# One-token attention with a 32768-long cache beside a SwiGLU FFN: own space for the projection weights, a broadcast q, earlier weight loads, and most of the output projection moved ahead

## The chip, the cores and the metric

The kernel runs on one core of one Trainium2 chip. The metric is the device time of one execution in microseconds (us), as a median over several executions. The profile is one execution, taken by the hardware profiler; its span is 1 to 2 us shorter than the timed figure. Engines in the profile: PE is TensorE (PEld its weight loads), DVE is VectorE, ACT is ScalarE, POOL is GpSimd, SP is SyncE, which here issues all transfers ("SPq" is its queue).

## The reference

One token, 32 heads with a K and a V cache of 32768 x 128 each in bf16, and a small FFN on the same normalised input:

```python
xn = _layernorm(x)                                   # x: [1, 1, 640]
q = (xn @ wq)                                        # wq: [640, 4096], 32 heads of 128
scores = einsum("bhqd,bhkd->bhqk", q, k) * 128**-0.5  # k, v: [1, 32, 32768, 128]
p = softmax(scores); o = einsum("bhqk,bhkd->bhqd", p, v)
att = o.reshape(1, 1, 4096) @ wo                     # wo: [4096, 640]
ffn = (silu(xn @ w_gate) * (xn @ w_up)) @ w_down     # 640 -> 1728 -> 640
out = x + att + ffn
```

K and V are 537 MB together, the weights 17 MB: 554 MB have to be read once.

## The kernel before

A head's K and V lie with 256 positions on each of 128 partitions. K comes in four chunks of 2 MB a head, into a ring of `KR = 6` slots; V in eight of 1 MB, into a ring of `VR = 8`. VectorE does q.k: a multiply with q broadcast over partitions, a tree of four folding additions in place, and a reduce. POOL reduces the maximum and the sum over partitions (a "partition all-reduce" each) and scales the maximum between the two, ScalarE takes exp, TensorE multiplies V (as weights) by p ("PV"). When a head's PV and its 1/sum are there, ScalarE copies the result out of PSUM, scaled by 1/sum (the "eviction").

```python
for i in range(NKC):                                  # VectorE; NKC = 128 chunks
    ...
    v.wait_ge(kdma[slot].sem, 16 * (i // KR + 1))
    dve_t.inc(v.tensor_tensor(out=kr, in0=kr, in1=qbh[...].to_broadcast(...), op=ALU.mult))
    for w in TREE:                                    # 64, 32, 16, 8
        ...
        dve_t.inc(v.tensor_tensor(out=kr[:, :, 0:w], in0=kr[:, :, 0:w], in1=kr[:, :, w:2 * w], op=ALU.add))
    v3 = dve_t.inc(v.tensor_reduce(out=scs[...], in_=kr[:, :, 0:TREE[-1]], axis=AX.X, op=ALU.add))
    if c == NCK - 1:
        head_ops(h)                                   # maximum of the head
        if h >= 1: rz_op(h - 1)                       # 1 / sum of the head before
        ...
```

wq and wo have no space of their own: wq lies in the first K slots at the start, wo in the same slots at the end. The in-order transfer queue shows what that means:

```python
wq_v = kflat[:, 0:NC_D * HQ * DH]...;  wo_v = kflat[:, 0:H * D]...     # kflat is the K ring
...
# SyncE: x, wq, FFN weights (in the V ring), then per K chunk i one K load and two V loads
if n_use > 0:             sp.wait_ge(dve_t.sem, NLVL * (i - KR + 1))   # the slot's last chunk is reduced
elif slot < KSLOTS_WQO:   sp.wait_ge(pe_a.sem, mile["qrows_last"])     # wq is used up
kdma[slot].inc(sp.dma_start(krings[:, slot, :], src))
if i == WO_POS:                                                        # WO_POS = NKC - 1, the last chunk
    sp.wait_ge(dve_t.sem, NLVL * (max(last_occ) + 1))
    c_wo.inc(sp.dma_start(wo_v[:, :, :], A_wo...))
...
sp.wait_ge(pe_pv.sem, q - VR + 1)                                      # V: its slot's PV is done
vdma[slot].inc(sp.dma_start(vrings[:, slot, :], src))
```

At the end, all 64 matmuls of the output projection follow the eviction of the last head (`t.wait_ge(act_ov.sem, H)`), then two additions and the output transfer.

## Time and profile before

| | before |
|---|---|
| time | 1374.21 us, 4 runs, 1373.22 to 1374.48 (13 runs later: 1373.63) |
| span of the profiled execution | 1372.5 us |
| VectorE busy | 1263.0 us, 92% |
| first multiply with K starts | 39.6 us |
| last reduce ends | 1313.5 us |
| from there to the end | 59.0 us |

The numbers to hold on to are the last three: the body, in which VectorE never rests, is framed by a head of 40 us and a tail of 59 us.

### The profile page before, as it was taken

What the parts mean: (1) busy time and instruction counts of PE and PEld (TensorE: products, weight loads), DVE (VectorE), ACT (ScalarE), POOL (GpSimd) and SP (SyncE); (2) the same over time, 40 slices, a digit from 0 to 9 for tenths busy, and PEclk for the clock granted to TensorE, in tenths of its full rate; (3) what the DMA queues carried; (4) which work ended last, traced back from release to release, by engine and by line L of the source; (5) the groups of instructions that cost most, each with busy time, mean ns of one, the idle gap of its engine ahead of it and who ended that gap; (6) DMA issues with size and microseconds to landing.
All of it is one profiled execution on the core that took longest, in us unless ns stands there. A gap on an engine that the chain in (4) does not pass through costs nothing.

```text
span 1372.5 us, 18658 instructions
## 1 busy us (share of the span) xinstructions
PE 263.4 (19%) x8474; PEld 242.2 (18%) x8474; DVE 1263.0 (92%) x858; ACT 28.6 (2%) x102; POOL 221.4 (16%) x101
## 2 busy tenths in 40 slices
PE   4220222222012222201222221022222102222105
PEld 2120222222012222201222221022222102222103
DVE  2899999999999999999999999999999999999920
ACT  0000000000000000000000000000000000000000
POOL 0021120121111111121110211111021121201200
PEclk9555555555555555555555555555555555555556
DMA  9999999999999999999999999999999999999474
GB/s 375 424 410 421 394 419 413 421 424 420 425 417 424 421 420 424 414 428 421 425 420 419 422 425 424 422 422 419 421 422 425 422 424 416 424 425 421 204 260 199
DMA packets 63283, 555.21 MB, mean 405 GB/s; under 512 B 6306, under 2 KB 12132, under 8 KB 13412
## 3 DMA queue, kind: packets, MB, share of 16 engines
q1 hardware_dynamic: 63204, 554.02, 96.8%
q8 instruction: 66, 1.08, 0.3%
q14 instruction: 13, 0.11, 0.0%
HBM read 553.99 MB, written 0.00 MB: 404 GB/s over the span
## 4 chain that ended last, share of the span: by engine, by line
DVE 91%; DMA 4%; PE 2%; issue 2%; SPq 1%; ACT 0%; DVEq 0%
DVE krings L359 44%; DVE krings L355 41%; DVE sc L362 6%; DMA vrings<-in_A_v_cache_dram 2%; DMA krings<-in_A_wq_dram 1%; DMA krings<-in_A_k_cache_dram 1%; PE psR L255 1%; PE psR L442 1%; SPq L496 1%; DVE rzb L343 0%; PE O L429 0%; SPq L462 0%; DVE pmax L337 0%; DVE rows L451 0%; DVE outb L453 0%
## 5 line engine op out<-in xcount | busy, mean ns | idle before, releaser
L359 DVE TENSOR_TENSOR krings<-krings 128x4096 bf16<-128x4096 bf16 (+3 forms) x512 | 593.0, 1158 | 17.5
L355 DVE TENSOR_TENSOR krings<-krings,qb 128x8192 bf16<-128x8192 bf16 x128 | 564.9, 4413 | 1.1 <-DMA krings<-in_A_k_cache_dram 1.1
L429 PE MATMUL O<-P,vrings 128*128 128x1 bf16 x8192 | 227.9, 165 | 1085.2 <-ACT P L403 993.3
L429 PEld LDWEIGHTS O<-P,vrings 128*128 128x128 bf16 x8192 | 223.1, 104 | 1090.1 <-ACT P L403 998.0
L379 POOL PARTITION_ALL_REDUCE gmaxb<-pmax x32 | 141.1, 4411 | 478.9 <-DVE pmax L337 478.9
L362 DVE TENSOR_REDUCE sc<-krings 128x64 f32<-128x512 bf16 x128 | 87.8, 686 | 4.4
L386 POOL PARTITION_ALL_REDUCE zb<-rowsum x32 | 43.6, 1364 | 276.6 <-issue 276.6
L382 POOL TENSOR_SCALAR negb<-gmaxb 128x1 f32<-128x1 f32 x32 | 34.1, 1065 | 329.7 <-issue 329.7
L403 ACT ACTIVATE P<-sc,negb 128x256 bf16<-128x256 f32 x32 | 16.3, 509 | 1263.8 <-POOL negb L382 1263.8
L451 DVE TENSOR_TENSOR rows<-rows 1x640 f32<-1x640 f32 x1 | 0.8, 812 | 34.3 <-PE psR L442 34.3
L343 DVE RECIPROCAL rzb<-zb 128x1 f32<-128x1 f32 x32 | 4.9, 153 | 20.7 <-POOL zb L386 20.7
L266 DVE CAST qrowb<-psR 1x512 bf16<-1x512 f32 x8 | 5.4, 678 | 14.2 <-PE psR L255 14.2
L337 DVE TENSOR_REDUCE pmax<-sc 128x1 f32<-128x256 f32 x32 | 13.4, 420 | 1.1
L255 PE MATMUL psR<-krings,xncol 128*1 128x512 bf16 x40 | 11.5, 459 | 7.6 <-DMA krings<-in_A_wq_dram 7.6
L442 PE MATMUL psR<-krings,ocol 128*1 128x320 bf16 x64 | 11.3, 350 | 0.4 <-ACT ocol L395 0.4
L297 DVE TENSOR_TENSOR sg<-sg,psG 128x13 f32<-128x13 f32 x1 | 0.2, 170 | 9.7 <-ACT sg L292 9.7
L395 ACT ACTIVATE ocol<-O,rzb 128x1 bf16<-128x1 f32 x32 | 7.9, 246 | 30.5 <-PE O L429 30.5
L442 PEld LDWEIGHTS psR<-krings,ocol 128*1 128x1 bf16 x64 | 6.1, 97 | 5.3 <-ACT ocol L395 0.4
L273 POOL PARTITION_BROADCAST qb<-qrowb x1 | 2.3, 2304 | 27.9 <-DVE qrowb L266 27.9
L255 PEld LDWEIGHTS psR<-krings,xncol 128*1 128x1 bf16 x40 | 3.8, 97 | 14.8 <-issue 11.5
L324 PE MATMUL psF<-vrings,hcol 128*1 128x320 bf16 (+1 forms) x28 | 5.9, 378 | 0.8 <-DVE hcol L303 0.8
L403 ACT ACTIVATION_READ_ACCUMULATOR P<-sc,negb 128x1 f32 x32 | 6.0, 188 | 0.0
(31 smaller groups left out, 26.6 us busy)
## 6 DMA issues: line engine op xcount, KB each, us to landing
krings<-in_A_k_cache_dram SPq DMA_DIRECT2D x128, 2048.0 KB, 25.6
vrings<-in_A_v_cache_dram SPq DMA_DIRECT2D x256, 1024.0 KB, 21.0
krings<-in_A_wq_dram SPq DMA_DIRECT2D x5, 1024.0 KB, 9.0
krings<-in_A_wo_dram SPq DMA_DIRECT2D x1, 5120.0 KB, 16.8
vrings<-in_B_w_gate_dram SPq DMA_DIRECT2D x1, 2160.0 KB, 17.4
vrings<-in_B_w_up_dram SPq DMA_DIRECT2D x1, 2160.0 KB, 22.2
vrings<-in_B_w_down_dram SPq DMA_DIRECT2D x1, 2080.0 KB, 27.6
vrings<-in_B_w_down_dram SPq DMA_DIRECT2D x1, 80.0 KB, 18.8
```

Source lines behind the costliest of these rows:

```text
L255: mm = t.matmul(psR[0:1, b % 2, 0:QB], lhsT=xncol[:, c:c + 1], rhs=wq_v[:, c, b * QB:(b + 1) * QB], start=(c == 0), stop=(c == NC_D - 1))
L337: v1 = dve_max.inc(v.tensor_reduce(out=pmax[:, b % SR:b % SR + 1], in_=scs, axis=AX.X, op=ALU.max))
L355: dve_t.inc(v.tensor_tensor(out=kr, in0=kr, in1=qbh[:, None, :].to_broadcast([128, CKK, DH]), op=ALU.mult))
L359: dve_t.inc(v.tensor_tensor(out=kr[:, :, 0:w], in0=kr[:, :, 0:w], in1=kr[:, :, w:2 * w], op=ALU.add))
L362: v3 = dve_t.inc(v.tensor_reduce(out=scs[:, c * CKK:(c + 1) * CKK], in_=kr[:, :, 0:TREE[-1]], axis=AX.X, op=ALU.add))
L379: v1 = pool_g.inc(g.partition_all_reduce(gmaxb[:, s:s + 1], pmax[:, s:s + 1], channels=128, reduce_op=ReduceOp.max))
L382: v2 = pool_neg.inc(g.tensor_scalar(out=negb[:, s:s + 1], in0=gmaxb[:, s:s + 1], scalar1=-c_scale, scalar2=None, op0=ALU.mult))
L386: v3 = pool_z.inc(g.partition_all_reduce(zb[:, s:s + 1], rowsum[:, s:s + 1], channels=128, reduce_op=ReduceOp.add))
L403: v1 = act_exp.inc(a.activation(out=P[:, b % PR, :], in_=sc[:, b % SCR, :], func=ACTF.Exp, bias=negb[:, b % SR:b % SR + 1], scale=c_scale, ...
L429: mm = t.matmul(ob[:, 0:1], lhsT=vrings[:, vslot, jj * DH:(jj + 1) * DH], rhs=P[:, pslot, j:j + 1], start=(j == 0), stop=(j == NJ - 1))
L442: mm = t.matmul(psR[0:1, b, 0:DBW], lhsT=ocol[:, h:h + 1], rhs=wo_v[:, h, b * DBW:(b + 1) * DBW], start=(h == 0), stop=(h == H - 1))
L496: vdma[slot].inc(sp.dma_start(vrings[:, slot, :], src))
```

## The change

The intent: K loads start right behind wq, the transfer queue no longer stands at wo near the end, and less work lies after the last V chunk. Cut to its core; the comments are added:

```diff
-    CKV = 32 if NJ >= 32 else NJ
+    CKV = 64 if NJ >= 64 else NJ          # V chunks of 2 MB
-    KR = 6
-    VR = 8
+    KR = 4
+    VR = 4
-    WO_POS = NKC - 1
+    WO_POS = min(KR - 1, NKC - 1)         # wo behind K chunk 3
+    FFNW_POS = min(1, NKC - 1)            # FFN weights behind K chunk 1
+        wqo = sbt("wqo", [128, WQO], BF16)   # wq, later wo: 40 KB per partition
-        qrowb = sbt("qrowb", [1, HQ * DH], BF16)
+        xnb = sbt("xnb", [128, NC_D, 128], BF16)
...  # q: xn broadcast to 128 columns as the stationary operand, so that every partition gets q
-                        mm = t.matmul(psR[0:1, b % 2, 0:QB], lhsT=xncol[:, c:c + 1], rhs=wq_v[...], ...)
+                        mm = t.matmul(QPS[b], lhsT=xnb[:, c, :], rhs=wq_v[...], ...)
-                mile["qb"] = pool_a.inc(g.partition_broadcast(qb[:, :], qrowb[0:1, :], channels=128))
...  # VectorE: the FFN's element-wise work after K chunks 1 and 3, not ahead of all
...  # TensorE, before PV of the last head
+                        if hp == H - 1:
+                            t.wait_ge(c_wo.sem, 16)
+                            t.wait_ge(act_ov.sem, H - 2)
+                            wo_rows(t, 0, H - 2)      # 60 of the 64 output matmuls
...  # SyncE
-                        elif slot < KSLOTS_WQO:
-                            sp.wait_ge(pe_a.sem, mile["qrows_last"])
...
                         if i == WO_POS:
-                            sp.wait_ge(dve_t.sem, NLVL * (max(last_occ) + 1))
+                            sp.wait_ge(pe_a.sem, mile["qblocks_last"])
                             c_wo.inc(sp.dma_start(wo_v, ...))
```

## The prediction

> **What bounds the kernel now.** I read the page's row of engines and 40 slices first, then the costliest groups, then the chain of waits, and then cut the span into stretches.
>
> ```profile
> PE 263.4 (19%) x8474; PEld 242.2 (18%) x8474; DVE 1263.0 (92%) x858; ACT 28.6 (2%) x102; POOL 221.4 (16%) x101
> ...
> DVE  2899999999999999999999999999999999999920
> ...
> DMA  9999999999999999999999999999999999999474
> ...
> L359 DVE TENSOR_TENSOR krings<-krings 128x4096 bf16<-128x4096 bf16 (+3 forms) x512 | 593.0, 1158 | 17.5
> L355 DVE TENSOR_TENSOR krings<-krings,qb 128x8192 bf16<-128x8192 bf16 x128 | 564.9, 4413 | 1.1 <-DMA krings<-in_A_k_cache_dram 1.1
> ```
>
> VectorE multiplies each 2 MB K chunk by q, folds it four times and reduces it. One chunk is 4.413 + 4 x 1.158 + 0.686 (the reduce's row) = 9.73 us, 9.82 with the gaps; four chunks and a head's small operations take 39.815 us (the maximum of head 0 starts at 79.01, that of head 31 at 1313.55: 1234.5/31). VectorE waits for a K chunk once, 1.1 us at the very start. So between 39.6 and 1313.5 us nothing but VectorE sets the time. But the DMA row is full as well: a head's K and V are 16.78 MB, and 16.78 MB in 39.815 us is 421.4 GB/s. The tail tells whether the transfers could go faster:
>
> ```profile
> 1287.00:1313.00 26.00, 5.28 (x192) 5.20 (x192) 25.49 (x18) 0.75 (x3) 3.33 (x2) 0.50 0.01 3
> 1314.00:1331.00 17.00, 0.00 (x0) 0.00 (x0) 0.04 (x1) 0.60 (x2) 0.63 (x2) 0.50 1.02 347
> 1331.00:1354.00 23.00, 8.08 (x256) 7.45 (x256) 0.16 (x1) 0.27 (x1) 0.40 (x1) 0.50 1.01 421
> 1354.00:1372.00 18.00, 13.35 (x128) 7.97 (x128) 1.62 (x2) 0.26 (x1) 0.00 (x0) 0.75 0.03 11
> ```
>
> The columns are stretch, length, then busy time and count of PE, PEld, DVE, ACT and POOL, clock, DMA share, GB/s. In the third stretch V alone streams with every other engine nearly idle: 421 GB/s. So the cap of the queue is about what VectorE asks for: two bounds within half a per cent. The first stretch is the waste: for 26 us before VectorE ends no byte moves, because the in-order DMA queue stands at the load of wo, which lives in the K ring and waits for the last K chunk:
>
> ```profile
> SPq L484 <- DVE sc L362: 56.5, 1, 56.5
> ```
>
> Ten V chunks (10.5 MB) and wo (5.2 MB) stand behind it and are loaded after VectorE has ended. The chain of waits shows it, and what comes after:
>
> ```profile
> 1313.55 0.38 SPq L484
> ...
> 1323.24 12.09 DMA vrings<-in_A_v_cache_dram
> ...
> 1336.42 20.08 DMA vrings<-in_A_v_cache_dram
> ...
> 1357.92 11.34 PE psR L442 x64
> ```
>
> The tail from the last reduce (1313.5) to the end (1372.5) is 59 us. The head of the kernel, 39.6 us, is the other loose part: the first K load waits until the q rows have left the K ring, because wq lies there.
>
> ```profile
> 16.07 11.49 PE psR L255 x40
> 27.59 11.91 DMA krings<-in_A_k_cache_dram
> 39.59 4.44 DVE krings L355
> ```
>
> **What the Trainium skill says.** "DMA: Bandwidth & Descriptors", section "Measured (HBM→SBUF, 128 partitions, SWDGE, issued from GpSimd)", gives 425 GB/s for 16 MB, one core alone. That path is another one, but this trace agrees: 421. The same page, "Why small descriptors are slow", names a fixed cost of about 3 cycles per packet; here 1280-byte rows (wo, w_down) are the slow ones: 347 GB/s in the second stretch against 421. "Perfetto Trace Analysis", "GPSIMD Engine Instruction", says to time POOL by start-to-start spacing; the recorded all-reduce lasts 0.37 us in the tail while the next POOL instruction starts 11.9 us after it (1314.08 to 1325.97), so I use spacings. "TensorE: Matmul & The Clock Gate", section "Wait — 56ns, not 53.3ns?", gives 426.7 ns cold and 215.7 warm for 512 moving columns, with no term for the number of stationary columns; the q rows here are spaced 0.43 us at first (weight loads at 16.45, 16.88, 17.31) and later run at 1.08 us for five.
>
> **The change, part by part.**
> 1. wq/wo get their own 40 KB per partition; the K ring shrinks from 6 to 4 slots. K loads follow wq at once. The order becomes wq, K0, K1, FFN weights, K2, K3, wo, K4, V0, K5, V1 and so on. In steady state each K is followed by one 2 MB V, as before by two of 1 MB.
> 2. q comes out broadcast over 128 partitions. The 40 matmuls still move 512 columns each, so about 11.5 us from 16.07; the eight 0.68 us evictions stay (128 partitions side by side). The last eviction ends at 27.59 + 0.68 = 28.3. The POOL broadcast (2.3 us) goes, but it was hidden under the wait for K0. A broadcast copy (estimate 0.5 us) falls before wq lands.
> 3. VectorE can start at 28.3 instead of 39.6: -11.3 us, if K0 is there. A 2.1 MB chunk at 421.5 GB/s takes 4.98 us; wq lands at 15.94, so K0 at 20.9 and K1 at 25.9. Both are early.
> 4. The FFN weights took 33.2 - 15.9 = 17.3 us, so they land at 43.2, K2 at 48.2, K3 at 53.2. wo landed 16.8 us after its issue, some 2 of them start-up: 14.9 us, so 68.1, and K4 at 73.1. On VectorE chunk 0 ends at 38.1, chunk 1 at 47.9. The FFN matmuls (4.4 us) end at 47.9 too, so the four FFN operations end at 49.0 (0.4 us wait, 0.7 work). Chunk 3 ends at 68.6, the ffn copy (0.8) and the maximum (0.5) bring 69.9. Chunk 4 then waits for K4 to 73.2: 3.3 us are given back to the early wo.
> 5. From there VectorE needs 31 heads x 39.815 = 1234.3 us, less 0.5 for what follows the last reduce: 1307.0. The transfers behind K4 up to the last K are 123 K + 123 V chunks, 246 x 4.98 = 1225 us, so K127 lands at 1298; VectorE needs it at 1297.2. A dead heat: I add 1.5 us of jitter. Last reduce at 1308.5, against 1313.5: the 11.3 shrink to 5.
> 6. Tail. Five V chunks follow K127, 24.9 us: the last lands at 1323. The chain of the last head in the old tail: last reduce 1313.5, maximum, all-reduce, exp at 1326.3, sum, reciprocal ended at 1334.94, which is 21.4 us. This did not show, as V came later; it becomes the end. Exp is at 1308.5 + 12.8 = 1321.3, its 256 PV matmuls (7 us) end at 1328.5, the reciprocal at 1329.9. Sixty of the 64 output matmuls run ahead, in the gap after head 30's PV (about 11 us, from about 1305); four remain (estimate 1.3 us). Then eviction 0.3, two additions 1.7, output transfer 1.5: 1329.9 + 4.9 = 1334.8.
>
> Sum against a span of 1372.5: -5 by the earlier VectorE end, -32.6 in the tail (59.0 to 26.3). Of the latter 10.6 are the matmuls moved ahead, the rest the V and wo transfers no longer queued behind the last K. The timed median lies 1.7 us above the span, so 1336.5 us, 2.7% less.
>
> **Rivals.** (a) The shallower ring starves VectorE. For: 8 MB of K instead of 12, and K landed at most 35 us after issue, while a ring of four gives only 3 x 9.8 = 29 us; the queue is also held in order behind V, which waits for PV of two heads ago (845.7 us of such waits in all). Against: that landing time is mostly the queue's own backlog; when VectorE waits for K, 25 to 35 us of transfers are queued, and V's slot comes free about 19 us after a head's end (the queue resumes at 257.7; head 4 ended at 79.0 + 4 x 39.8 = 238.3). If the DMA still idled 1 us a head, 32 us come back and the result is about 1368, the same. At 0.3 us a head it would be 1346. (b) The DMA becomes the bound and its rate decides: at 419 instead of 421.5 the stream takes 7.5 us more, so 1344; at 424, by packets of 16 instead of 8 KB for V, VectorE binds again and only the jitter goes: 1335. The share of 1.01 in every steady stretch speaks for a DMA without room. (c) Of the two gains only the start counts because the tail stays bound by V, say if V of the last head waits for head 30's PV behind the 60 matmuls: +5 to 8 us, 1343. (d) Wo early does not delay K4, or the exp chain is faster: 1332 at best.
>
> **Range and chances.** The floor is VectorE without any wait after 28.3: 1332 timed. Rivals (b) and (c) give 1343 or 1344, a part of (a) 1348. So 1330 to 1348 for 8 in 10. The line of 2% is 1346.7: faster 0.87, within 2% 0.12, slower 0.01.
>
> **What would show it.** First K multiply at about 28; a VectorE wait for K of 3 to 4 us near 70 and small ones after; no stretch at 0 GB/s before the last reduce, which ends near 1308; eviction of the last head 21 us later, set by POOL's sum rather than by V; four matmuls and 4.9 us to the end. Wrong if VectorE's waits for K sum to over 10 us, if the DMA idles each head, or if the head period leaves 39.8.

## The result, and the profile after

The changed kernel takes 1333.32 us (8 runs, 1332.29 to 1334.18) against 1373.63 us (13 runs) for the kernel before: ratio 0.9705, 95% interval 0.9695 to 0.9714. A ratio is the mean time of one kernel's fast runs over that of the other's of the same rounds, so it is not quite the ratio of the medians.

| | before | predicted | after |
|---|---|---|---|
| first multiply with K | 39.6 | 28.3 | 28.56 |
| chunk 4 starts, after a wait for K4 of | no wait | 73.2, 3.3 | 73.40, 3.33 |
| last reduce ends | 1313.5 | 1308.5 | 1306.8 |
| exp of the last head | 1326.3 | 1321.3 | 1319.7 |
| its PV ends | 1357.6 | 1328.5 | 1327.3 |
| its 1/sum is there | 1334.9 | 1329.9 | 1326.5 |
| span | 1372.5 | 1334.8 | 1332.1 |
| time | 1374.2 | 1336.5 | 1333.3 |

The page of the changed kernel: the rows of VectorE and the transfers in 40 slices, and VectorE's multiply with its idle time and the releaser.

```profile
DVE  4989999999999999999999999999999999999993
...
DMA  9999999999999999999999999999999999999994
...
L356 DVE TENSOR_TENSOR krings<-krings,qb 128x8192 bf16<-128x8192 bf16 x128 | 564.9, 4413 | 4.0 <-DMA krings<-in_A_k_cache_dram 3.9
```

VectorE is full from the second slice to the last but one; the multiply takes the same 4413 ns, and VectorE waits for K for 3.9 us in all. Now the head in VectorE's timeline (start, length, engine, line, operation, count, and in brackets the idle time before it and who ended it):

```profile
27.84 0.69 DVE L269 CAST qb<-ps 128x512 bf16<-128x512 f32 x1 [0.39 <-PE ps L259]
28.56 4.42 DVE L356 TENSOR_TENSOR krings<-krings,qb 128x8192 bf16<-128x8192 bf16 x1
...
49.29 4.42 DVE L356 TENSOR_TENSOR krings<-krings,qb 128x8192 bf16<-128x8192 bf16 x1 [0.60 <-DMA krings<-in_A_k_cache_dram]
...
73.40 4.42 DVE L356 TENSOR_TENSOR krings<-krings,qb 128x8192 bf16<-128x8192 bf16 x1 [3.33 <-DMA krings<-in_A_k_cache_dram]
```

The 11 us of the earlier start are there, and 3.9 us of them are paid back at chunks 2 and 4. The tail, stretch by stretch (columns as in the prediction):

```profile
1287.00:1313.00 26.00, 16.24 (x279) 11.42 (x277) 19.94 (x15) 0.00 (x0) 1.05 (x2) 0.58 0.94 389
1300.00:1320.00 20.00, 12.96 (x124) 7.64 (x124) 7.11 (x8) 0.33 (x1) 0.63 (x2) 0.76 0.63 258
1320.00:1332.00 12.00, 8.21 (x260) 7.24 (x260) 1.79 (x3) 0.69 (x4) 0.40 (x1) 0.50 0.01 4
```

The stretch from 1287 to 1313 us, in which nothing was moved before, runs at 389 GB/s, and after 1320 us nothing is left to move. What sets the end is in the timeline of the tail:

```profile
1306.11 0.69 DVE L363 TENSOR_REDUCE sc<-krings 128x64 f32<-128x512 bf16 x1
...
1307.35 0.37 POOL L382 PARTITION_ALL_REDUCE gmaxb<-pmax  x1 [13.28 <-DVE pmax L338]
1319.38 0.26 POOL L385 TENSOR_SCALAR negb<-gmaxb 128x1 f32<-128x1 f32 x1 [11.66 <-issue]
1319.67 0.51 ACT L406 ACTIVATE P<-sc,negb 128x256 bf16<-128x256 f32 x1 [33.54 <-POOL negb L385]
...
1320.33 6.98 PE L442 MATMUL ps<-P,vrings 128*128 128x1 bf16 x256 [6.13 <-ACT P L406]
1325.89 0.40 POOL L389 PARTITION_ALL_REDUCE zb<-rowsum  x1 [6.25 <-issue]
1326.32 0.17 DVE L344 RECIPROCAL rzb<-zb 128x1 f32<-128x1 f32 x1 [19.00 <-POOL zb L389]
1327.35 0.26 ACT L398 ACTIVATE ocol<-ps,rzb 128x1 bf16<-128x1 f32 x1 [6.93 <-PE ps L442]
```

("issue" is put where the engine waited for nothing that the profile shows.) After the last reduce, 12 us pass on POOL between the all-reduce of the maximum and its scaling; then exp, and 256 PV matmuls without a wait for V. The eviction follows PV by 0.04 us; 1/sum has been there for 0.9 us.

### The profile page after: what moved, and what is told of

The parts are those of the page before. It is cut to its first block, busy times and chain, and to the rows that moved or that the text cites.

```text
span 1332.1 us, 18530 instructions
## 1 busy us (share of the span) xinstructions
PE 270.5 (20%) x8474; PEld 245.7 (18%) x8474; DVE 1263.8 (95%) x859; ACT 28.5 (2%) x102; POOL 204.5 (15%) x100
## 2 busy tenths in 40 slices
DMA packets 44850, 555.19 MB, mean 417 GB/s; under 512 B 4258, under 2 KB 10084, under 8 KB 11364
## 3 DMA queue, kind: packets, MB, share of 16 engines
q8 instruction: 66, 1.08, 0.3%
## 4 chain that ended last, share of the span: by engine, by line
DVE 91%; DMA 3%; issue 3%; SPq 3%; PE 1%; POOL 0%; ACT 0%; POOLq 0%
DVE krings L360 44%; DVE krings L356 40%; DVE sc L363 6%; DMA krings<-in_A_k_cache_dram 3%; SPq L474 1%; SPq L477 1%; PE ps L442 1%; SPq L473 0%; DVE rzb L344 0%; SPq L469 0%; DVE pmax L338 0%; PE ps L418 0%; SPq L493 0%; DVE rows L458 0%; DVE outb L460 0%
## 5 line engine op out<-in xcount | busy, mean ns | idle before, releaser
L356 DVE TENSOR_TENSOR krings<-krings,qb 128x8192 bf16<-128x8192 bf16 x128 | 564.9, 4413 | 4.0 <-DMA krings<-in_A_k_cache_dram 3.9
L442 PE MATMUL ps<-P,vrings 128*128 128x1 bf16 x8192 | 233.6, 165 | 1027.8 <-ACT P L406 692.9
L442 PEld LDWEIGHTS ps<-P,vrings 128*128 128x128 bf16 x8192 | 225.8, 104 | 1035.9 <-ACT P L406 695.9
L382 POOL PARTITION_ALL_REDUCE gmaxb<-pmax x32 | 136.3, 4260 | 484.1 <-DVE pmax L338 484.1
L389 POOL PARTITION_ALL_REDUCE zb<-rowsum x32 | 30.9, 966 | 298.6 <-issue 298.6
L269 DVE CAST qb<-ps 128x512 bf16<-128x512 f32 x8 | 5.5, 692 | 13.5 <-PE ps L259 13.5
L259 PE MATMUL ps<-wqo,xnb 128*128 128x512 bf16 x40 | 11.7, 467 | 7.6 <-DMA wqo<-in_A_wq_dram 7.6
L418 PE MATMUL ps<-wqo,ocol 128*1 128x320 bf16 x64 | 12.4, 367 | 0.4 <-ACT ocol L398 0.4
L398 ACT ACTIVATE ocol<-ps,rzb 128x1 bf16<-128x1 f32 x32 | 7.8, 244 | 6.9 <-PE ps L442 6.9
L418 PEld LDWEIGHTS ps<-wqo,ocol 128*1 128x1 bf16 x64 | 6.2, 99 | 5.7 <-ACT ocol L398 0.4
L259 PEld LDWEIGHTS ps<-wqo,xnb 128*128 128x128 bf16 x40 | 4.5, 115 | 14.4 <-issue 11.6
L323 PE MATMUL ps<-vrings,hcol 128*1 128x320 bf16 (+1 forms) x28 | 6.1, 383 | 1.4 <-DVE hcol L302 1.4
```

Source lines behind the costliest of these rows:

```text
L259: mm = t.matmul(QPS[b], lhsT=xnb[:, c, :], rhs=wq_v[:, c, b * QB:(b + 1) * QB], start=(c == 0), stop=(c == NC_D - 1))
L356: dve_t.inc(v.tensor_tensor(out=kr, in0=kr, in1=qbh[:, None, :].to_broadcast([128, CKK, DH]), op=ALU.mult))
L382: v1 = pool_g.inc(g.partition_all_reduce(gmaxb[:, s:s + 1], pmax[:, s:s + 1], channels=128, reduce_op=ReduceOp.max))
L389: v3 = pool_z.inc(g.partition_all_reduce(zb[:, s:s + 1], rowsum[:, s:s + 1], channels=128, reduce_op=ReduceOp.add))
L418: mm = t.matmul(psR[0:1, b, 0:DBW], lhsT=ocol[:, h:h + 1], rhs=wo_v[:, h, b * DBW:(b + 1) * DBW], start=(h == 0), stop=(h == H - 1))
L442: mm = t.matmul(ob[:, 0:1], lhsT=vrings[:, vslot, jj * DH:(jj + 1) * DH], rhs=P[:, pslot, j:j + 1], start=(j == 0), stop=(j == NJ - 1))
```

## The experiments

My theory after the result: two chains meet at the end. VectorE runs without rest from 28.6 us but for 3.9 us; behind its last reduce comes maximum, POOL, exp, PV, eviction. The rival: 554 MB at 421 to 426 GB/s are 1301 to 1316 us, so the transfers set the end, and the rest is slack.

**1. The 64 output matmuls after the eviction again.**

```diff
                         if hp == H - 1:
-                            t.wait_ge(c_wo.sem, 16)
-                            t.wait_ge(act_ov.sem, H - 2)
-                            wo_rows(t, 0, H - 2)
+                            pass
...
-                mm = wo_rows(t, H - 2, H)
+                mm = wo_rows(t, 0, H)
```

> The changed kernel with all 64 output matmuls after the last eviction again. My theory: they stand on the path that sets the end, so the time rises by what the old 64 took less what the new 4 take, 11.3 - 1.2 = 10.1 us, to about 1343.4 us; eviction of the last head stays at about 1327.3 us of the span. Rival (the last transfers or the sum on POOL hide the matmuls): 1333 to 1336 us.

Measured: 1343.34 us, 10.0 us more; eviction of the last head at 1327.27. The theory holds, the moved matmuls are worth what they took (10.85 against 1.23 us).

**2. V in chunks of 1 MB.**

```diff
-    CKV = 64 if NJ >= 64 else NJ
+    CKV = 32 if NJ >= 32 else NJ
-    VR = 4
+    VR = 8
```

> The changed kernel with V in chunks of 1 MB, eight slots, as before (8 KB rows). My theory: the 425 to 426 GB/s of the changed kernel against 421 before come from the 16 KB rows of V; so this run streams at 421 to 422 GB/s between 100 and 1300 us, VectorE's waits for K grow from 3.9 to 5 to 8 us, and the time is 1334 to 1337 us. Rival (the higher rate is only the stream running ahead of VectorE at a cap that was always there): 425 GB/s, K waits of 4 us, 1333 us.

Measured: 1334.61 us (ratio to before 0.9718, interval 0.9704 to 0.9733, which overlaps with the changed kernel's), 423 GB/s between 100 and 1300 us against 425, waits for K 4.7 us, of which 4.4 at chunk 4; last reduce at 1307.8. So neither: the rate falls by half of what I said, and VectorE notices only at chunk 4. The size of the V chunks is worth about 1 us or nothing.

**3. K loads wait for the q matmuls.**

```diff
                             sp.wait_ge(dve_t.sem, NLVL * (i - KR + 1))
+                        elif i == 0:
+                            sp.wait_ge(pe_a.sem, mile["qblocks_last"])
```

> The changed kernel, but the first K load waits for the last q matmul, as before. My theory: the queue stands idle from about 16 to 28 us; K0 lands at about 35, the FFN weights at 57, K4 at 87 instead of 73.4, and VectorE runs without slack from there, so the whole 13.6 us come through: 1347 us. Rival (the start is slack, as the prediction's net 5 us suggests, and later stretches absorb it): 1333 to 1338 us.

Measured: 1346.06 us, 12.7 more; last reduce 13.6 later (1320.4); waits for K 11.1 us. The rival falls: no later stretch absorbs a late start. (The kernel before was better off than this run, as it filled the pause with the FFN weights. Run 10 undoes the order alone.)

**4. wo behind chunk 100.**

```diff
-    WO_POS = min(KR - 1, NKC - 1)
+    WO_POS = min(100, NKC - 1)
```

> The changed kernel with the wo load behind K chunk 100 instead of K chunk 3. My theory: the wait of 3.3 us for K4 near 70 us goes, and by chunk 100 the stream is so far ahead of VectorE that 15 us of wo do not stop it; last reduce at 1303.5, time 1330.0 us. Rival (the stream has no room, the same 5.2 MB stop VectorE wherever they are): VectorE waits 3 us or more near chunk 101 to 105 and the time is 1333 us or above.

Measured: 1337.24 us, slower than the changed kernel; my theory was wrong. VectorE's waits for K between 1000 and 1100 us:

```profile
DVE krings L356 <- DMA krings<-in_A_k_cache_dram: 6.0, 3, 5.3
```

The columns are sum, times and longest. Without wo at chunk 3, K landed 17.7 us after its issue (median between 300 and 500 us), against 28.3 in the changed kernel; a ring of four allows 3 x 9.8 = 29.5, so the stream led VectorE by 10 to 12 us. But it never gained on VectorE (19.3 us between 900 and 1000), so about 15 us of wo exceed a lead of this size at any chunk, and the issue of the next V load was held for 16.75 us behind wo as well.

**5. wo right behind the last K chunk.**

```diff
-    WO_POS = min(KR - 1, NKC - 1)
+    WO_POS = NKC - 1
```

> The changed kernel with the wo load right behind the last K chunk, in its own buffer, without a wait. Theory after the run with wo at chunk 100: the stream leads VectorE by about 10 us and never gains on it, so 15 us of wo cost VectorE time anywhere before the last K, and nothing behind it. The wait near 70 us goes, last reduce at 1303.5, V of the last head still lands before its exp (1317), time 1330.0 us. Rival (wo pushes V of the last head beyond its exp, the same bytes bind at the end): last reduce 1303.5 but the PV matmuls wait for V, time 1333 to 1340 us.

Measured: 1332.52 us (ratio 0.9705, as the changed kernel; the profiled execution is the slowest of the four, 1335.34). The last reduce ended at 1303.44, as expected, yet nothing was won, and the rival's mechanism is in the timeline of the tail:

```profile
1306.15 1.87 PE L442 MATMUL ps<-P,vrings 128*128 128x1 bf16 x64 [18.18 <-DMA vrings<-in_A_v_cache_dram]
...
1316.66 0.51 ACT L406 ACTIVATE P<-sc,negb 128x256 bf16<-128x256 f32 x1 [33.88 <-POOL negb L385]
...
1326.82 1.86 PE L442 MATMUL ps<-P,vrings 128*128 128x1 bf16 x64 [3.06 <-DMA vrings<-in_A_v_cache_dram]
```

The last V chunk of head 30 waits behind wo and is used only at 1306; its slot takes the last chunk of head 31, which lands at 1326.8, 10 us after exp. Here the transfers set the end, but by little: 1/sum was there at 1326.1, because POOL took 21.5 us between its two all-reduces (18.5 in the changed kernel), and so the end would have come about 2.5 us earlier without the wait for V.

**6. No maximum for the last head.** It takes head 30's maximum as its shift, which leaves the softmax the same unless exp overflows: for the experiment, not for use on any input.

```diff
-                        head_ops(h)
+                        if h < H - 1:
+                            head_ops(h)
...  # POOL: for the last head only the sum
...  # ACT: b == H - 1 takes negb of b - 1, and waits for the last reduce
-                        if hp == H - 1:
+                        if hp == H - 2:          # 58 output matmuls before PV of head 30
```

> The changed kernel, where the last head takes the maximum of the head before as its shift (exact for a softmax as long as exp does not overflow), so no maximum, all-reduce and scaling stand between the last reduce and its exp; 58 output matmuls are moved to before PV of head 30 and 6 remain. Theory: the 12.5 us from the maximum to exp are on the path that sets the end; without them exp starts at 1307, and V of the last head (landing at 1313 to 1316) or the POOL sum (about 1314) comes last: eviction at 1316 to 1318, time 1322 to 1325 us. Rival (V of the last head lands only at 1321 to 1323, as the prediction had it, so that the transfers bind): eviction at 1324 to 1326, time 1330 to 1333 us.

Measured: 1328.55 us (ratio 0.9672), between the two. Exp started at 1306.6, and the POOL sum took 0.4 us and was there at 1307.7, which I had not expected. PV then waited for V three times; its last chunk:

```profile
1314.79 1.86 PE L452 MATMUL ps<-P,vrings 128*128 128x1 bf16 x64 [2.99 <-DMA vrings<-in_A_v_cache_dram]
1319.67 1.86 PE L452 MATMUL ps<-P,vrings 128*128 128x1 bf16 x64 [3.02 <-DMA vrings<-in_A_v_cache_dram]
```

So POOL's 12.5 us were on the path, but only 5 us deep; then V binds. The stretches of this run show how it binds (the last two columns are the mean share of the 16 DMA engines, and GB/s):

```profile
1309.00:1312.00 3.00, 2.00 (x70) 1.83 (x66) 0.00 (x0) 0.00 (x0) 0.00 (x0) 0.50 0.74 311
1312.00:1315.00 3.00, 0.21 (x8) 0.21 (x9) 0.00 (x0) 0.00 (x0) 0.00 (x0) 0.50 0.23 98
1315.00:1318.00 3.00, 1.65 (x62) 1.57 (x59) 0.00 (x0) 0.00 (x0) 0.00 (x0) 0.50 0.11 44
1318.00:1321.00 3.00, 1.33 (x50) 1.34 (x51) 0.00 (x0) 0.00 (x0) 0.00 (x0) 0.50 0.01 5
```

From 1312 us most DMA engines have nothing left, and still the last chunk lands at 1319.7. A share of 0.11 is that of about two engines of 16. The reading that fits is that a few engines lag by some 6 us, that the chunk is complete only when they are done, and that the mean rate hides it. It is not shown engine by engine: the views have only the mean.

**7. The kernel before, with wo apart.** This and run 9 take the change apart from the other end.

```diff
-    KR = 6
+    KR = 4
+        wob = sbt("wob", [128, H * D], BF16)
-        wo_v = kflat[:, 0:H * D].rearrange("p (h n) -> p h n", h=H)
+        wo_v = wob[:, :].rearrange("p (h n) -> p h n", h=H)
-                            sp.wait_ge(dve_t.sem, NLVL * (max(last_occ) + 1))
```

> The kernel before with one thing changed: wo has its own buffer and is loaded right behind the last K chunk without waiting for VectorE (K ring 4 slots to make room). Theory: the idle 26 us of the queue go, VectorE still ends at 1313.5; the end is then set by exp at 1326.3, PV to 1333.3, the sum to 1335, and all 64 output matmuls after it: span 1350, time 1351.5 us; that is 22 us of the 40 us. Rival (the ring of 4 starves VectorE in the body): last reduce 1318 or later and the time 1356 us or above.

Measured: 1345.96 us, 27.6 less than before. The last reduce stays at 1313.5; the end came 5 us earlier than I had said, as POOL took 8.0 us instead of 12 between all-reduce and scaling, which nothing in the edit explains. The pause at wo was more than half of the gain.

**8. A K ring of three** (with wo at the end).

```diff
-    KR = 4
+    KR = 3
```

> The run with wo at the end, with three K slots instead of four. Tests how much room the ring has. Theory: with the lead of about 10 us, K landed 18 us after its issue; a ring of three gives 2 x 9.8 = 19.6 us, just enough, so VectorE's waits for K sum to less than 8 us and the time is 1330 to 1338 us. Rival (a shallow ring starves VectorE once a head, when the queue is held behind V): 1 us or more a head, 1360 us or above.

Measured: 1332.12 us (run 5: 1332.52); VectorE waits for K 1.1 us in the whole run; K lands 10 us after its issue. The lead of about 10 us is in the transfers and not in the number of slots.

**9. Run 7 with the output matmuls moved ahead.**

```diff
                     if c == 0:
+                        if hp == H - 1:
+                            ...                   # waits as in the changed kernel
+                            wo_rows(t, 0, H - 2)
                         t.wait_ge(act_exp.sem, hp + 1)
```

> The kernel before with wo apart (the run of that name, 1346.0 us), and 60 of the 64 output matmuls moved ahead of the last head's PV. Theory: what is left of the change is then only the earlier start; the matmuls are worth 10 us here too, so 1336 us (up to 1340 if POOL's all-reduce takes 12 us in the tail instead of the 8 us of that run). Rival (V of the last head binds, so that the hoist gives nothing): 1342 to 1346 us.

Measured: 1337.95 us, 8.0 less than run 7: the 10 us less 1.4 by which POOL's sum came later, and V's last chunk came into sight (PV waited 0.3 us for it).

**10. The changed kernel with the FFN weights ahead of K0.**

```diff
-                ffn_issued = False
+                ffn_weight_dmas()
+                ffn_issued = True
```

> The changed kernel with the FFN weights loaded before K0 as in the kernel before (wq still outside the K ring, nothing waits). The same bytes move without a pause, only the order differs. Theory: K0 lands at 38.2, VectorE starts there instead of at 28.6, chunk 4 starts at 79.6 instead of 73.4 and there is no wait for K4; VectorE and the exp chain behind it set the end, so the 6.2 us come through: 1339.5 us, last reduce at 1313. Rival (the transfers set the end, and they are the same): 1333 to 1335 us.

Measured: 1338.77 us, 5.5 more. VectorE started at 39.55 after 11.6 us of waiting, chunk 4 at 80.3, the last reduce ended at 1313.7. The same bytes in another order cost 5.5 us: at this place VectorE's chain sets the end and not the number of bytes.

**11. More instructions for TensorE.** A guess at why some DMA engines lag.

```diff
                     v = pe_pv.inc(mm)
+                    if hp < H - 2:
+                        for _ in range(32):
+                            t.matmul(psA[:, 0:1], lhsT=xnb[:, 0, :], rhs=xncol[:, 0:1], start=True, stop=True)
```

> The changed kernel with 32 idle matmuls (on constant operands, into a free bank) after each V chunk of heads 0 to 29: 3840 more matmuls, so about half as many PE instructions again, which are fetched by DMA. Hypothesis: at the end of the changed kernel the mean DMA share falls to 0.12 and 0.06 while V still lands, so one or two of the 16 engines lag by 6 to 8 us; if it is the fetch of PE's instructions (1.08 MB) that holds them up, half as much again makes them lag 3 to 4 us more, VectorE's waits for K rise from 3.9 to 6 us or more, and the time by 2 to 5 us. Rival (the lag has another cause): waits for K and time within 1.5 us of the changed kernel, 1333 us.

Measured: 1333.39 us, waits for K 4.6 us, while the instruction queue moved 1.57 MB instead of 1.08. The guess falls; the cause of the lag is open.

**12. The scaling of the maximum on ScalarE.** Run 6 had shown a partition all-reduce that takes 0.4 us. Why, then, 12 us before the scaling and 6 before the sum? POOL's queue gives a hint. These are the lines of the scaling and of the sum in the changed kernel (count; least, median and greatest duration in ns; first and last start):

```profile
L385 POOLq MODIFY_POOL_CONFIG  x64: 83/83/83, 70.4 to 1307.7; - x64
L389 POOLq MODIFY_POOL_CONFIG  x64: 11/11/11, 80.6 to 1320.0; - x64
```

Twice 64 for 32 heads: at each turn from all-reduce to scaling and back, POOL's configuration is modified. The Trainium skill, "GPSIMD Engine Reference", section "2.1 Instruction dispatch", says that this instruction can load code, and that the "first call to a freshly-loaded kernel additionally pays an IRAM-load of approximately 6 µs", without a visible instruction. In the tail of the changed kernel the turn to the sum agrees (from the last change at 1320.0 to 1325.89: 5.9 us), the turn to the scaling does not (1307.7 to 1319.38: 11.7 us). So leave POOL only one kind of work:

```diff
-                    v2 = pool_neg.inc(g.tensor_scalar(out=negb[...], in0=gmaxb[...], scalar1=-c_scale, ...))
...  # ACT
-                    a.wait_ge(pool_neg.sem, b + 1)
+                    a.wait_ge(pool_g.sem, b + 1)
+                    v0 = pool_neg.inc(a.activation(out=negb[...], in_=gmaxb[...], func=ACTF.Copy, scale=-c_scale))
+                    a.wait_ge(pool_neg.sem, v0)
```

> The changed kernel with one operation of each head moved: the scaling of the maximum by -1/sqrt(128) goes from POOL to ScalarE, so POOL runs nothing but all-reduces after the start. Hypothesis: the 12 us between all-reduce and scaling and the 6 us between scaling and the sum are not the reductions (0.4 us in the run without the last maximum) but POOL changing its loaded code at each switch, twice a head; so exp of the last head starts 2 to 3 us after the last reduce instead of 12.9, the last V chunk (landing 1318 to 1320) sets the end as it did in the run without the last maximum, and the time is 1327 to 1329.5 us with the exact maximum kept. Rival (the gap is the all-reduce itself, or POOL held up by VectorE): exp stays 8 us or more behind the last reduce and the time is 1331 us or above.

Measured: 1323.31 us (5 runs, 1322.89 to 1323.4), ratio to before 0.9634, interval 0.9621 to 0.9648: the fastest of all, 10 us ahead of the changed kernel, and more than I had expected. The tail:

```profile
1306.06 0.69 DVE L363 TENSOR_REDUCE sc<-krings 128x64 f32<-128x512 bf16 x1
...
1307.30 0.35 POOL L382 PARTITION_ALL_REDUCE gmaxb<-pmax  x1 [32.94 <-DVE pmax L338]
1307.68 0.20 ACT L402 ACTIVATE negb<-gmaxb 128x1 f32<-128x1 f32 x1 [34.66 <-POOL gmaxb L382]
1307.91 0.51 ACT L405 ACTIVATE P<-sc,negb 128x256 bf16<-128x256 f32 x1
...
1308.61 0.38 POOL L385 PARTITION_ALL_REDUCE zb<-rowsum  x1 [0.96 <-ACT P L405]
...
1316.31 0.26 ACT L394 ACTIVATE ocol<-ps,rzb 128x1 bf16<-128x1 f32 x1 [7.65 <-PE ps L441]
```

What is left of configuration changes in POOL's queue are two at the very start, at the line of the first all-reduce:

```profile
L382 POOLq MODIFY_POOL_CONFIG  x2: 11/11/11, 0.8 to 0.8; - x2
```

From the last reduce to exp are 1.2 us instead of 12.9. The all-reduce of the sum, which the edit does not touch, starts 0.1 us after the row sums are there (1308.52) instead of 5.6. So the gaps come with the alternation and its configuration changes, and not with the reductions; that the time goes into loading code is what the skill says, and no trace here shows the load itself. And V came earlier too: PV hardly waited after exp (0.7 us, not put down to V), and the eviction came at 1316.3, while in run 6 the last chunk landed at 1319.7. K's median time from issue to landing falls from 28.0 us (100 to 400 us) over 25.4 (500 to 800) to 22.6 (900 to 1250), where it stays at 28 in the changed kernel. So here the stream gains on VectorE. Fewer code loads among the transfers, or V slots that come free earlier in each head, could both be the reason. The traces speak for the slots: between 100 and 1250 us the in-order queue stood 272.8 us at V loads that waited for PV in the changed kernel, and 2.4 us here, while the DMA queues moved the same bytes (555.19 and 555.18 MB). No run separates the two.

## Why the prediction was right, and where it was off

- **The head.** First multiply, FFN weights, wait for K4: each within half a us. Run 10 confirms the link from there to the end. The prediction gives no source for the 2 us of start-up that it takes off wo, nor for the 0.5 us of the broadcast copy; the copy took 0.82 us and was done before wq landed.
- **The body.** Right that VectorE sets it, at 39.8 us a head. The 1.5 us of jitter for a dead heat with the transfers were the mis-sized term: after chunk 4 VectorE never waited, and the last reduce came at 1306.8, 0.2 us from the sum without them. The cap of 421.5 GB/s was too low for V chunks of 2 MB (425 to 426 GB/s in the body), and the lag at the end of the stream (run 6), not in the prediction at all, means that a mean rate does not tell when a chunk lands.
- **The tail.** Predicted 26.3 us, measured 25.3. The prediction let 1/sum come 1.4 us after PV; it came 0.8 us before the end of PV, as POOL's spacings were shorter (18.5 us between the two all-reduces, 20.3 before). So PV and not 1/sum set the eviction, by 0.9 us. The matmuls moved ahead: 10.6 predicted, 10.0 in run 1; the 10.6 is 60/64 of the old 11.34 us, but the prediction's own 1.3 us for the four that stay leaves 10.0. The miss of 2.7 us in the span is 1.7 from the body and 1.0 from the tail; nothing cancelled.
- **The 12 us on POOL.** The prediction took the spacing for the length of the all-reduce. The number was right and its meaning was not: in the tail the all-reduce takes 0.35 us (4.5 in the heads, beside a busy VectorE), and run 12 removed the rest. That the old tail's 11.9 us from all-reduce to scaling came again (12.0) was luck: runs 7 and 8, which do not touch POOL, have 8.0 and 7.9.
- **The rivals.** (a) fell most clearly: VectorE waited 3.9 us in all, and with wo at the end even three slots are enough (run 8). Of (b) the second branch came: 425 GB/s, and the jitter gone. Run 2, with 8 KB rows again, streams at 423 and costs 1 us or nothing, so the rows account for about half of the step from 421. (d) fell: wo delayed K4 by 3.3 us, and exp came 12.9 us after the last reduce (12.8 predicted). (c) did not happen: the 60 matmuls ended at 1314.2, 5.5 us before exp. Run 5 shows (c) where wo is loaded late.
- **The sum.** From before: wo apart 27.6 us (run 7), matmuls ahead 8.0 (run 9), the earlier start and the rest 4.6 (1337.95 less 1333.32): 40.3 together. Taken out of the changed kernel singly, the matmuls count 10.0 and the start 5.5, as what each saves depends on which chain comes last. The parts are good to a few us only: POOL's time between the two all-reduces of the tail runs from 15.5 us (run 7) to 21.5 (run 5) in runs that do not touch POOL; 4.8 of the 27.6 us are such a difference (15.5 against 20.3 before).

## What to carry to other kernels

Ask of every weight that shares a buffer with a stream what stands in the in-order queue behind its load: here 26 us without a byte, which showed as a wait of SyncE and as a 4 in the DMA row, not as a wait of the bound engine. When a tail shrinks, what lay beside it becomes the tail: give each chain behind the last bound instruction its own sum before you count the gain. And where POOL alternates between two kinds of operation, look for configuration changes in its queue and try to give one kind to another engine: here that was worth 10 us.

## What the Trainium skill lacked or had wrong

- "GPSIMD Engine Reference", section "2.1 Instruction dispatch": it gives about 6 us for the first call after a code load, and does not say that ordinary operations can bring a configuration change at every turn. Here the configuration changes recur twice a head, and POOL sits idle for 6.25 us before the sum and 11.66 us before the scaling in the tail of the changed kernel, 7.3 to 11.6 and 7.4 to 12.3 us in its heads.
- No page has the time of a one-column partition all-reduce: 0.35 to 0.40 us with VectorE idle (run 12 and run 6), 4.5 us for the maximum beside a busy VectorE (median of run 12).
- "DMA: Bandwidth & Descriptors", section "Latency and other measured facts", has two engines slower than the others and calls that, as a best guess, specific to SWDGE. Here all loads go through the hardware queue, and the mean share still falls to 0.23 and 0.11 in the two stretches from 1312 to 1318 us, while the last V chunk is under way (run 6). Whether single engines lag, and which, the runs don't show.
- The same page has no figure for how long a load of many short rows holds the issuer: a V load is issued in 0.33 us, but in 16.75 us right behind wo, which has 4096 rows of 1280 bytes (run 4). That the rows are the reason is not tested.
